# Attention kernel with a weight decode on the side: VectorE's per-head work merged, the decode dealt out by time, seven products on GpSimd

## The chip, the core and the metric

The kernel runs on one core of one Trainium2 chip. The metric is the device time of one execution in microseconds (us), lower is better. Before the change three runs took 588.17, 589.28 and 589.59 us, so the median is 589.28 us.

The engines have short names here as in the profile: PE is TensorE (PEld its weight loads), DVE is VectorE, ACT is ScalarE, POOL is GpSimd, and SP is the engine whose queue issues most DMAs. PSUM is the memory that PE writes its results to, SBUF the main on-chip memory.

## What is computed

Three stages follow each other: an attention with queries pooled in pairs, a mixture of experts in which each token goes to one expert, and a two-layer network. The change touches the first stage and the decode of the weights for the third, which runs beside it.

```python
q_pool = q.reshape(B, H, S // 2, 2, D).mean(axis=3)          # B, H, S, D = 2, 8, 1152, 64
scores = scale * np.matmul(q_pool, k.transpose(0, 1, 3, 2))
scores = scores - np.max(scores, axis=-1, keepdims=True)
attn = np.exp(scores)
attn = attn / (np.sum(attn, axis=-1, keepdims=True) + 1e-09)
x = np.matmul(attn, v)                                        # heads side by side: 1152 tokens x 512
...
skip_score = x @ w_skip ; logits = xc @ w_gate ; e_idx = np.argmax(logits, axis=1)
y[mask] = gate_w[mask, None] * (np.maximum(xc[mask] @ w1[e], 0.0) @ w2[e])
...
h = x @ w_in ; g = h * np.tanh(softplus(h)) ; out = g @ w_out
```

The weights `w_in` and `w_out` arrive in 64-bit numbers. They are turned into 32-bit numbers on the chip, in 32 blocks of 128x512, with integer operations on the high and the low word. This is called the decode here.

## The kernel before

**The iterations.** The attention is a software pipeline of 72 iterations: 8 heads of 9 tiles of 128 queries, and 9 more iterations to run out. `pos` is the number of the iteration within its head (0 to 8), and the tile at `pos` 4 is put together from half tiles of both batches. All work is issued by one Python loop (from line 349) in a fixed order, and each engine runs its own instructions strictly in that order. There is no scheduler.

One iteration `n` issues the following, in this order:

- `turn`: PE transposes the tile of iteration n-3 in 64-column pieces. Eight of nine key blocks go to the PSUM tile `tp`, the ninth to the last columns of `ov`.
- `finish` (only at `pos` 7, for the head before) or `av_step`: PE multiplies transposed weights with the values, two or three of the 18 steps of a head, into the two banks of `ov`. The first nine steps (group 0) fill bank 0, the last nine (group 1) bank 1.
- `ext_copy` (only at `pos` 3): ACT copies the value sums of group 0 out of `ov`. Those of group 1 are copied by DVE inside `av_step`, at `pos` 6.
- `expo`: ACT takes the exponential of the tile of iteration n-1 and sums it.
- `put_e`: ACT copies the transposed pieces out of PSUM. The part from `tp` is issued by `turn`, the part from `ov` after `expo`.
- `scores`: PE computes the scores of tile n into the PSUM tile `s` (4 banks, one buffer). DVE then reads all of `s`, scales it, writes it to SBUF and keeps the extreme value of each row (line 147). This is the eviction, and the next scores wait for its end.
- `dec_run`: DVE gets some operations of the decode.

**`finish`** takes the sums of a finished head (`ext`), multiplies them on PE with a matrix that holds an identity and the gate weights (lines 249 and 256), and DVE divides by the sums of the exponentials (lines 267 and 273, two batches apart). The reciprocals come from `norm`, issued at `pos` 3 of the next head. `logits` adds the gate columns up.

**The decode** of a block has five operations. `first` issues a product of the high word with itself on POOL and a shift on DVE. Two more DVE operations of two inputs each follow (lines 318 and 319), and `last` (line 313) multiplies by the test that the product is not tiny. `DECS` says by `pos` how many operations an iteration gets; in the iteration in which a head's value sums are complete it gets none. Blocks are loaded two ahead from HBM (`dec_load`, first in iteration 6) and stored by SP when the next block begins (`dec_store`). `beside` makes a POOL operation wait for the last score product of the iteration, so that it begins together with the eviction. POOL also adds the query pairs (`q_sum`, two per head).

## Time and profile before

| | |
|---|---|
| median of three runs | 589.28 us (588.17 to 589.59) |
| the profiled execution, its own time | 585.41 us |
| its span, first to last instruction | 583.6 us |
| granted TensorE clock, mean | 0.985 of full speed |
| busy: PE, PEld | 544.4 us (93%), 400.2 us (69%) |
| busy: DVE, ACT, POOL | 376.1 us (64%), 357.5 us (61%), 73.8 us (13%) |
| eviction (line 147), 72 times | 97.7 us, mean 1357 ns |
| exponential (line 158), 72 times | 90.5 us, mean 1257 ns |
| POOL product of the decode (line 307), 32 times | 34.4 us, mean 1075 ns |

The attention fills the first 245 us or so of the span. DVE and ACT are busiest there; the rest is ruled by PE and, in the mixture of experts, by the weight DMAs. A busy PE is not PE at its peak, because matrix products are pipelined and their ends are modelled. The profile says for each idle stretch what ended it, as far as semaphores tell. Where the engine named had long been done, something else ended it.

### The profile page before, as it was taken

Reading aid. Unit: us, or ns where it says so; the run is one execution under the profiler, and the core shown is the slowest. Engines: PE = TensorE matmul, PEld = TensorE weight load, DVE = VectorE, ACT = ScalarE, POOL = GpSimd, SP = SyncE. Lnnn points to the kernel's source line nnn. Section 1 sums busy time; section 2 is a strip of 40 time slices with the busy share of each in tenths; the row PEclk is TensorE's granted clock in tenths of the full one; section 3 lists DMA queues with packets and bytes.
Section 4 is the critical chain, followed back from the end, with each engine's and each line's share of the span. In section 5 each row is a group of like instructions: output and inputs, shape, how many; then the busy total and the mean of one; then the engine's idle time right before and its main releaser. Section 6 shows DMA issues by size and latency. Waiting matters only on the chain. (4 is left out here: it accounts for less than half of the span.)

```text
span 583.6 us, 11993 instructions
## 1 busy us (share of the span) xinstructions
PE 544.4 (93%) x4745; PEld 400.2 (69%) x4745; DVE 376.1 (64%) x731; ACT 357.5 (61%) x663; POOL 73.8 (13%) x82
## 2 busy tenths in 40 slices
PE   6799999999999998779989979999999999999994
PEld 3566666666566665436644645889889999898983
DVE  3588888888888887250010026599987667766663
ACT  3878878788778887202112013599978666676662
POOL 1313231322232220033000100000000000000000
PEclk9999999999999999889998989999999999999998
DMA  8594969798849771029999195346211300010001
GB/s 262 190 311 165 343 210 354 231 326 280 295 140 353 243 269 45 19 83 338 402 361 384 53 342 195 111 148 229 61 36 58 106 2 1 0 56 1 1 0 58
DMA packets 50388, 102.99 MB, mean 176 GB/s; under 512 B 14075, under 2 KB 15483, under 8 KB 50320
## 3 DMA queue, kind: packets, MB, share of 16 engines
q1 hardware_dynamic: 47792, 95.99, 47.7%
q0 software_dynamic: 1296, 3.75, 2.0%
q10 hardware_dynamic: 1232, 2.36, 1.2%
q8 instruction: 41, 0.67, 0.5%
q14 instruction: 27, 0.22, 0.1%
HBM read 85.49 MB, written 17.04 MB: 176 GB/s over the span
## 5 line engine op out<-in xcount | busy, mean ns | idle before, releaser
L147 DVE TENSOR_SCALAR_CACHE_REDUCE scp<-s 128x1152 f32<-128x1152 f32 x72 | 97.7, 1357 | 31.5 <-PE s L144 18.8
L1046 PE MATMUL ph<-xT,wi 128*128 128x384 f32 x576 | 108.5, 337 | 0.0
L1046 PEld LDWEIGHTS ph<-xT,wi 128*128 128x128 f32 x576 | 102.2, 188 | 4.2
L144 PE MATMUL s<-ks,qs 64*128 64x288 f32 (+1 forms) x640 | 89.3, 427 | 8.9 <-DVE scp L147 7.3
L158 ACT ACTIVATE scp<-scp,mx 128x1152 f32<-128x1152 f32 x72 | 90.5, 1257 | 11.2 <-DVE scp L147 10.7
L1100 PE MATMUL po<-wo,gh 128*128 128x512 f32 x288 | 90.3, 394 | 0.8 <-ACT gh L1085 0.6
L206 PE MATMUL ov<-eT,vt 128*64 128x288 f32 x576 | 84.3, 422 | 1.2 <-ACT eT L188 1.2
L188 ACT COPY eT<-tp 128x1024 f32<-128x1024 f32 x64 | 65.0, 1016 | 27.3 <-PE tp L174 27.3
L144 PEld LDWEIGHTS s<-ks,qs 64*128 64x128 f32 (+1 forms) x640 | 48.6, 176 | 44.8 <-DVE scp L147 15.6
L1100 PEld LDWEIGHTS po<-wo,gh 128*128 128x128 f32 x288 | 52.9, 188 | 10.3 <-ACT gh L1085 1.5
L1100 PE MATMUL po<-wo,gl 128*128 128x512 f32 x144 | 57.2, 397 | 0.0
L174 PEld LDWEIGHTS tp<-cst,scp 64*128 64x128 f32 x1152 | 46.9, 138 | 13.7 <-ACT eT L188 3.8
L1070 ACT ACTIVATE u<-u 128x384 f32<-128x384 f32 (+1 forms) x49 | 25.4, 519 | 46.6 <-DVE u L1064 46.1
L1090 DVE TENSOR_TENSOR gl<-s,gh 128x384 fp32r<-128x384 f32 (+1 forms) x49 | 27.0, 550 | 41.7 <-ACT gh L1085 41.5
L206 PEld LDWEIGHTS ov<-eT,vt 128*64 128x64 f32 x576 | 36.6, 138 | 23.0 <-issue 1.4
L307 POOL TENSOR_TENSOR g<-wd 128x512 f32<-128x512 f32 x32 | 34.4, 1075 | 131.6 <-PE s L144 96.3
L174 PE MATMUL tp<-cst,scp 64*128 64x64 f32 x1152 | 48.1, 223 | 0.6 <-ACT eT L188 0.6
L1100 PEld LDWEIGHTS po<-wo,gl 128*128 128x128 f32 x144 | 27.0, 187 | 6.7 <-DVE gl L1090 1.0
L1072 ACT ACTIVATE r<-s,one 128x384 f32<-128x384 f32 (+1 forms) x49 | 30.0, 612 | 1.6
L1071 ACT ACTIVATE s<-u,one 128x384 f32<-128x384 f32 (+1 forms) x49 | 29.9, 610 | 1.6
L1064 DVE TENSOR_SCALAR u<-ph 128x384 f32<-128x384 f32 (+1 forms) x49 | 26.7, 546 | 6.5 <-PE ph L1046 6.4
L1079 DVE SCALAR_TENSOR_TENSOR r<-u,r 128x384 f32<-128x384 f32 (+1 forms) x49 | 26.9, 550 | 1.7
(180 smaller groups left out, 656.3 us busy)
## 6 DMA issues: line engine op xcount, KB each, us to landing
w<-w SPq DMA_DIRECT2D x32, 1024.0 KB, 10.9
wd<-wq SPq DMA_DIRECT2D x32, 512.0 KB, 5.1
wdec<-g SPq DMA_DIRECT2D x32, 256.0 KB, 5.1
vt<-vt SPq DMA_DIRECT2D x8, 576.0 KB, 4.4
ks<-kt SPq DMA_DIRECT2D x15, 288.0 KB, 7.2
ring<-wdec SPq DMA_DIRECT2D x16, 256.0 KB, 4.6
wr<-wdec SPq DMA_DIRECT2D x16, 256.0 KB, 2.8
xr<-qt SPq DMA_DIRECT2D x7, 576.0 KB, 4.7
```

Source lines behind the costliest of these rows:

```text
L144: st["tick"] = nc.tensor.matmul(s[o, half, j, :HQ], w[r], st["k", h, b][r, cs], start=True, stop=True).ins
L147: nc.vector.tensor_scalar(scp.rearrange("p (a c) -> p a c", a=4), s.rearrange("p a j c -> p (a j) c")[:, :, :HQ], -EXP_SCALE, -NEG, op0=AL ...
L158: nc.scalar.activation(scp, scp, AF.Exp, bias=mx, scale=-1.0, accum_out=st["sum", h][:, t : t + 1],)
L174: nc.tensor.matmul(to, e[q, P * i : P * i + P], io["ident"][q, q], start=i < 8 or a != opened, stop=True, is_transpose=True, skip_group_ch ...
L188: nc.scalar.copy(to.rearrange("p k (a c) -> p a k c", a=2), v)
L206: nc.tensor.matmul(acc[D * b : D * b + D, :288], st["v", h][:, b, kc], src[:, kc, b], start=(kc == 0), stop=(kc == KC - 1), skip_group_che ...
L307: beside(nc.gpsimd.tensor_tensor(g, hf, hf, op=ALU.mult))
L1046: nc.tensor.matmul(ph, wi.w[i][:, a, P * k : P * k + P], xTs[c][b][:, k], start=(n == 0), stop=(n == 11),)
L1071: nc.scalar.activation(s[:, c], u[:, c], AF.Square, bias=one)
L1072: nc.scalar.activation(r[:, c], s[:, c], AF.Ln, bias=one)
L1090: nc.vector.tensor_tensor(gl[:, c], a["t"][1][:, c], gh[:, c].bitcast(F32), op=ALU.subtract)
L1100: nc.tensor.matmul(acc[j], g[a][:, P * j : P * j + P], wo[b][:, i], start=(i == 0 and n == 0), stop=(i == 15 and n == 2),)
```

## The change

Five things change in the attention; the stages behind it are the same.

- In `finish` the two batches are divided by one DVE instruction that reads both banks of `ov`, and the four half tiles go to one bank so that one instruction divides them too. `norm` is called in `finish` and no longer at `pos` 3. For the last head ACT has nine columns to scale and not ten.
- `ext_copy` is issued behind `expo` and `put_e`.
- The decode is dealt out by time: each operation has a cost in us (0.45, 0.72, 0.28 for `logits`), and an iteration gives out operations as long as they fit into `SPARE[pos]`. It also does so in the iterations that run out. The first blocks are loaded in iteration 3, not 6.
- For the seven blocks of `OFF` the last operation is not DVE's. POOL does the test and the product, as two instructions.
- POOL's operations are queued in `side` and issued one per iteration. Before a `last`, and before the store of a block of `OFF`, all of them are issued at once.

```diff
-DECS = (2, 2, 2, 2, 2, 2, 2, 3, 3)
+SPARE = (1.45, 1.45, 1.9, 1.45, 1.45, 0.75, 0.0, 1.75, 1.45)
+OFF = (5, 9, 13, 17, 21, 25, 29)
...
         def finish(h):
             st.pop(("v", h))
+            norm(h)
...
-                        xp[b][D * b + 32 * g : D * b + 32 * g + 32, 4 * XW : 5 * XW], ext[q, g, 256:], wb[q],
+                        xp[0][D * b + 32 * g : D * b + 32 * g + 32, 4 * XW : 5 * XW], ext[q, g, 256:], wb[q],
...
-            for b in range(B):
-                nc.vector.tensor_tensor(
-                    xt[:, 5 * b : 5 * b + 4, lo:],
-                    xp[b][:, : 4 * XW].rearrange("p (t c) -> p t c", t=4)[:, :, lo:],
-                    r[:, 5 * b : 5 * b + 4].unsqueeze(2).to_broadcast([P, 4, XW - lo]), op=ALU.mult,
-                )
-                q, x, c = cols[8 + b]
-                nc.vector.tensor_scalar(xt[q, c, lo:], x[:, lo:], r[q, c : c + 1], None, op0=ALU.mult)
...
+            nc.vector.tensor_tensor(
+                xt.rearrange("p (b t) c -> p b t c", b=B)[:, :, :4, lo:],
+                ovs[:, :, : 4 * XW].rearrange("p b (t c) -> p b t c", t=4)[:, :, :, lo:],
+                r.rearrange("p (b t) -> p b t", b=B)[:, :, :4].unsqueeze(3).to_broadcast([P, B, 4, XW - lo]),
+                op=ALU.mult,
+            )
+            nc.vector.tensor_scalar(xt[:, 4, lo:], cols[8][0][:, lo:], r[:, 4:5], None, op0=ALU.mult)
...
             def first():
-                beside(nc.gpsimd.tensor_tensor(g, hf, hf, op=ALU.mult))
+                side.append(lambda: tt(g, hf, hf, op=ALU.mult))
...
+            def third():
+                sts(x1, hb, 0xC0000000, x1, op0=ALU.bitwise_and, op1=ALU.bitwise_or)
+                if i in OFF:
+                    side.append(lambda: nc.gpsimd.tensor_scalar(g, g, W_TINY * W_TINY, None, op0=ALU.is_ge))
+                    side.append(lambda: tt(g, g, x1.bitcast(F32), op=ALU.mult))
+                    dec_out.append((i, g))
+
             def last():
+                while side:
+                    beside(side.pop(0)())
...
-        def dec_run(n):
-            for _ in range(n):
-                if not dec_ops and dec:
+        def dec_run(spare):
+            while dec or dec_ops:
+                if not dec_ops:
...
+                if dec_ops[0][0] > spare:
+                    return
+                cost, op = dec_ops.pop(0)
+                spare -= cost
+                op()
...
         def dec_store():
             if dec_out:
+                while side and dec_out[0][0] in OFF:
+                    beside(side.pop(0)())
...
-            if n % 9 == 3 and n > 9:
-                norm(n // 9 - 1)
...
-            if pos == 3 or not run:
-                ext_copy()
             if 0 < n <= nseq:
                 expo(*seq[n - 1])
             if trn:
                 put_e(*seq[m], slice(8, KC), ovs[:, :, c].unsqueeze(2))
+            if pos == 3 or not run:
+                ext_copy()
...
-                if n == 6:
+                if n == 3:
                     dec_load(0)
                     dec_load(1)
...
-            if run and not fin:
-                dec_run(DECS[pos])
-            if run and sums and (not st["used"] or pos + len(sums) > 8):
-                beside(q_sum(h + 1, sums.pop(0), slice(0, Q), nc.gpsimd))
+            if not fin:
+                dec_run(SPARE[pos] if run else 1.45)
+            if run and not st["used"]:
+                if sums and pos + len(sums) > 7:
+                    beside(q_sum(h + 1, sums.pop(0), slice(0, Q), nc.gpsimd))
+                elif side:
+                    beside(side.pop(0)())
+                elif sums:
+                    beside(q_sum(h + 1, sums.pop(0), slice(0, Q), nc.gpsimd))
```

The order of the instructions is shown at three places. Line numbers of the changed kernel differ a little: its eviction is line 148, its exponential 159, the copies out of PSUM 186 and 189, the copies of the value sums 214 (DVE) and 224 (ACT).

ACT at `pos` 3 of the second head, before: `ext` are the value sums, `eT` the transposed weights, `scp` the scores of a tile.

```order
L188 COPY eT<-tp 128x2x8x64
L223 COPY ext<-ov 128x288
L158 ACTIVATE scp,sums<-scp,mx 128x1152
L188 COPY eT<-ov 128x128
L188 COPY eT<-tp 128x2x8x64
```

And ACT at the same place with the change:

```order
L189 COPY eT<-tp 128x2x8x64
L159 ACTIVATE scp,sums<-scp,mx 128x1152
L189 COPY eT<-ov 128x128
L224 COPY ext<-ov 128x288
L189 COPY eT<-tp 128x2x8x64
```

The copy of the value sums has moved from ahead of the exponential to behind the small copy out of `ov`.

DVE at `pos` 6 to 8 of the third head, where the second head is finished, before: `xt` is the divided output, `r` the reciprocals, `x_...` and `g` belong to the decode.

```order
L213 COPY ext<-ov 128x288
L147 TENSOR_SCALAR scp,mx<-s 128x1152
L267 TENSOR_TENSOR xt<-ov,r 128x292
L273 TENSOR_SCALAR xt<-ov,r 64x73
L267 TENSOR_TENSOR xt<-ov,r 128x292
L273 TENSOR_SCALAR xt<-ov,r 64x73
L147 TENSOR_SCALAR scp,mx<-s 128x1152
L286 TENSOR_TENSOR lg<-lg,xt 128x81
L318 SCALAR_TENSOR_TENSOR x_1021<-wd,x_1021 128x512
L319 SCALAR_TENSOR_TENSOR x_1021<-wd,x_1021 128x512
L147 TENSOR_SCALAR scp,mx<-s 128x1152
```

And DVE at the same place with the change:

```order
L214 COPY ext<-ov 128x288
L148 TENSOR_SCALAR scp,mx<-s 128x1152
L231 TENSOR_SCALAR r<-sums 128x9
L232 RECIPROCAL r<-r 128x9
L265 TENSOR_TENSOR xt<-ov,r 128x2x292
L271 TENSOR_SCALAR xt<-ov,r 128x73
L148 TENSOR_SCALAR scp,mx<-s 128x1152
L284 TENSOR_TENSOR lg<-lg,xt 128x81
L307 TENSOR_SCALAR x_1017<-wd 128x512
L326 SCALAR_TENSOR_TENSOR x_1017<-wd,x_1017 128x512
L148 TENSOR_SCALAR scp,mx<-s 128x1152
```

Four divisions became two, with the two small instructions of `norm` ahead of them. The block that begins here is one of `OFF`: DVE has no last operation for it.

DVE in the first head, before, where the decode begins behind the seventh eviction:

```order
L107 TENSOR_TENSOR qs_138<-xr 128x288
L147 TENSOR_SCALAR scp,mx<-s 128x1152 x7
L308 TENSOR_SCALAR x_306<-wd 128x512
L318 SCALAR_TENSOR_TENSOR x_306<-wd,x_306 128x512
L147 TENSOR_SCALAR scp,mx<-s 128x1152
```

And with the change:

```order
L108 TENSOR_TENSOR qs_138<-xr 128x288
L148 TENSOR_SCALAR scp,mx<-s 128x1152 x4
L307 TENSOR_SCALAR x_214<-wd 128x512
L326 SCALAR_TENSOR_TENSOR x_214<-wd,x_214 128x512
L148 TENSOR_SCALAR scp,mx<-s 128x1152
```

The first operation on a loaded block (`wd`) now stands ahead of the fifth eviction instead of the eighth. On SP the loads of the first three blocks stand where they stood, behind the keys, queries and gate weights of the second head.

## Rows read from the trace of the kernel before

**Rows 1.** Busy time by stage, 74 to 104 us: length, PE, PEld, DVE, ACT, POOL, PEclk, DMA, GB/s

```profile
74.00:104.00 30.00, 29.48 (x372) 19.60 (x370) 26.28 (x46) 24.15 (x41) 8.40 (x7) 1.00 0.80 286
```

**Rows 2.** Timeline of PE, score products at `pos` 8: start us, us, what [idle before]

```profile
29.07 1.24 PE L144 MATMUL s<-ks,qs 64*128 64x288 f32 x8
...
57.76 1.24 PE L144 MATMUL s<-ks,qs 64*128 64x288 f32 x8
...
85.50 1.24 PE L144 MATMUL s<-ks,qs 64*128 64x288 f32 x8
...
226.09 1.24 PE L144 MATMUL s<-ks,qs 64*128 64x288 f32 x8
```

**Rows 3.** Timeline of DVE at `pos` 8 and 0 of the fifth head

```profile
145.70 0.69 DVE L313 SCALAR_TENSOR_TENSOR g<-g,x 128x512 f32<-128x512 f32 x1
146.31 1.35 DVE L147 TENSOR_SCALAR_CACHE_REDUCE scp<-s 128x1152 f32<-128x1152 f32 x1
```

**Rows 4.** Timeline of ACT and PE at `pos` 3 and 4 of the fourth head

```profile
97.49 0.40 ACT L223 COPY ext<-ov 128x288 f32<-128x288 f32 x1 [0.66 <-PE ov L206]
97.79 1.26 ACT L158 ACTIVATE scp<-scp,mx 128x1152 f32<-128x1152 f32 x1
98.21 0.76 PEld L174 LDWEIGHTS tp<-cst,scp 64*128 64x128 f32 x16
...
99.04 0.25 ACT L188 COPY eT<-ov 128x128 f32<-128x128 f32 x1
...
99.34 0.14 PEld L174 LDWEIGHTS ov<-cst,scp 64*128 64x128 f32 x2 [0.37 <-ACT eT L188]
```

**Rows 5.** Timeline of DVE, ACT and PE at `pos` 7 of the fourth head

```profile
109.74 0.46 DVE L267 TENSOR_TENSOR xt<-ov,r 128x292 f32<-128x292 f32 x1 [0.60 <-PE ov L256]
110.15 0.29 DVE L273 TENSOR_SCALAR xt<-ov,r 64x73 f32<-64x73 f32 x1
...
110.36 0.76 PEld L174 LDWEIGHTS tp<-cst,scp 64*128 64x128 f32 x16
...
110.82 0.30 DVE L273 TENSOR_SCALAR xt<-ov,r 64x73 f32<-64x73 f32 x1
...
111.21 0.33 ACT L185 COPY eT<-ov 128x64 f32<-128x64 f32 x2 [0.63 <-DVE xt L273]
...
111.58 0.14 PEld L174 LDWEIGHTS ov<-cst,scp 64*128 64x128 f32 x2 [0.46 <-ACT eT L185]
```

**Rows 6.** Timeline of ACT, PE and DVE where the attention runs out

```profile
231.00 0.40 ACT L223 COPY ext<-ov 128x288 f32<-128x288 f32 x1 [2.12 <-PE ov L206]
...
235.75 6.00 PE L206 MATMUL ov<-eT,vt 128*64 128x288 f32 x36 [1.21 <-ACT eT L188]
...
244.70 0.68 DVE L313 SCALAR_TENSOR_TENSOR g<-g,x 128x512 f32<-128x512 f32 x1
```

**Rows 7.** Busy time by stage, 232 to 240 us, columns as in rows 1

```profile
232.00:236.00 4.00, 1.30 (x22) 1.02 (x24) 0.39 (x2) 3.06 (x7) 0.00 (x0) 0.90 0.01 4
236.00:240.00 4.00, 4.00 (x24) 2.04 (x24) 0.00 (x0) 0.00 (x0) 0.00 (x0) 0.67 0.00 0
```

**Rows 8.** Timeline of SP: first load of the decode is issued

```profile
12.44 0.71 SPq L296 DMA_DIRECT2D wd<-wq  x1
```

**Rows 9.** DMA issues of 12.44 to 13.1 us: count, KB each, us to landing

```profile
wd<-wq SPq DMA_DIRECT2D x1, 512.0 KB, 7.9
```

**Rows 10.** Timeline of DVE, the fifth eviction of the first head

```profile
18.64 1.36 DVE L147 TENSOR_SCALAR_CACHE_REDUCE scp<-s 128x1152 f32<-128x1152 f32 x1 [1.49 <-ACT scp L158]
```

**Rows 11.** Timeline of DVE and POOL where their operations overlap

```profile
33.24 0.69 DVE L313 SCALAR_TENSOR_TENSOR g<-g,x 128x512 f32<-128x512 f32 x1
33.25 1.58 POOL L307 TENSOR_TENSOR g<-wd 128x512 f32<-128x512 f32 x1 [5.15 <-PE s L144]
...
102.04 1.41 POOL L107 TENSOR_TENSOR qs<-xr 128x576 f32<-128x576 f32 x1 [2.29 <-issue]
...
103.31 0.69 DVE L319 SCALAR_TENSOR_TENSOR x<-wd,x 128x512 uint32<-128x512 uint32 x1
```

More of the change, by code (lines that the diff above doesn't have):

```diff
@@ L316, in dec_step @@
             dec_ops.extend((
[L317 to L325 removed]
+                (0.45, first),
+                (0.72, lambda: sts(x1, lb, 29, x1, op0=ALU.logical_shift_right, op1=ALU.bitwise_or)),
+                (0.72, third),
+            ))
+            if i not in OFF:
+                dec_ops.append((0.72, last))
+        side = []
+        def dec_run(spare):
+            while dec or dec_ops:
+                if not dec_ops:
                     i = dec[0][0]
@@ L411, in attention @@
             finish(pend.pop(0))
-        while dec or dec_ops:
-            dec_run(1)
+        dec_run(1e9)
         while dec_out:
```

21 lines of the change are left out of this document (7 added, 14 removed).

## The prediction

> **What bounds the kernel now.** I read the busy time by stage first. In the attention PE is busy for 29.48 of 30 us, DVE for 26.28 and ACT for 24.15 [rows 1]. That says little by itself, since a wait of a few tenths between pipelined products hardly shows. So I went to the timeline and took the start of the score products as the clock of the loop: every iteration has one, and the next cannot start before DVE has evicted this one. The 63 iterations from 29.07 to 226.09 us take 197.02 us, 28.15 us per head of nine. One of these seven heads, from 57.76 to 85.50 us, takes only 27.74 [rows 2]. The reader should see in this that a head has a fixed part, the same in all heads, and a part that comes and goes. I looked for both.
>
> The part that comes and goes is DVE. At `pos` 8 of the fifth head the third decode operation begins at 145.70, and the eviction behind it starts only when it is through, at 146.31 [rows 3]. The scores that it takes were ready 0.6 us earlier.
>
> The fixed part holds two waits of PE. At `pos` 4 the transposes into `ov` wait 0.37 us for ACT's small copy [rows 4]. ACT is late because at `pos` 3 it stood idle for 0.66 us until PE was through with the value products, copied the sums for 0.40 us, and only then took the exponential, at 97.79. At `pos` 8 the same transposes wait 0.46 us for ACT again, and ACT waits 0.63 us for DVE's four divisions [rows 5]. After these waits are taken off, PE works without a gap, so I take PE's own work as the floor.
>
> **The sum, part by part.** All times are of the profiled execution, 585.41 us, which is 0.66% below the median of 589.28. I take the difference off the median.
>
> *Copy of the value sums.* Behind the change the exponential can start when ACT became idle, 97.49 less 0.66 = 96.83, its copy follows 1.25 later (97.79 to 99.04) at 98.08, and the sums are copied by about 98.75. PE's transposes into `ov` can follow those into `tp`, whose loads end at 98.21 + 0.76 = 98.97. So the wait of 0.37 goes, and what is late next is nothing: 0.2 us are left between the copy and the transposes. Seven heads have it: -2.6 us.
>
> *Merged divisions.* The chain runs from 109.74 to 111.12. 292 columns cost 0.46 and, by the eviction (1152 columns in 1.36), each further column about 1 ns; 584 columns then cost about 0.76. The second instruction starts 0.05 before the first ends, as now, and takes 0.3: the end is at 110.75, 0.37 earlier. `norm` is two instructions on nine columns. Two divisions of 73 columns bound them at 0.6, and DVE is idle for 0.60 just ahead of this chain, waiting for PE, so they cost nothing; without that cover they would cost up to 0.4. With ACT 0.37 earlier, PE's wait of 0.46 shrinks to about 0.1. Seven heads: -2.6 us.
>
> *Decode by time.* An iteration now gets at most two decode operations between evictions, 1.44 us in all. With the eviction's 1.36 that is 2.8 us, and an eviction and its scores alone (1.36 and 1.24, one after the other) already need 2.6 and their hand-overs, about 2.8. Nothing in a head then makes an eviction late, and each head runs like the best one: 197.02 - 7 x 27.74 = 2.8 us. Seven of 32 last operations leave DVE, 0.69 each, but that time is idle time now and adds nothing. Taken: -2.8 us. The bounds are 0 and -2.8.
>
> *Running out.* At 231.00 the sums were copied after ACT had been idle for 2.12 us, and the last exponential stood behind the copy [rows 6]. It fits into that idle time. Its 1.26 us leave the chain, of which PE's transposes give back some 0.25: the last value products start 1.0 earlier than 235.75. Their 6.00 us hold a second loss. PE was busy for only 1.30 of the 4 us before, the granted clock fell from 1.00, and from 236 to 240 its mean was 0.67, between the levels of 2.4 and 1.2 GHz, with PE busy throughout: 4 x 0.33 = 1.3 us [rows 7]. With a gap shorter by one microsecond I expect the clock to hold: -1.3, bounds 0 and -1.5. At the end DVE has no decode operation left ahead of the routing (0.68 at 244.70), two divisions less and ACT one column less, but DMAs of the output rows run beside: -0.5, bounds -0.2 and -0.9. Together -2.8 us.
>
> *Earlier start of the decode.* This one costs. SP issues the first load of the decode at 12.44 [rows 8], in a queue whose order the change keeps up to there, and it lands 7.9 us later, at 20.34 [rows 9]. Before, its first reader on DVE stood behind the seventh eviction and never waited. Now that reader stands in DVE's queue ahead of the fifth eviction, which started at 18.64 [rows 10]. The eviction waits for the load and for two operations (0.46 and 0.6 from start to start), until 21.4: +2.8 us, and PE, ACT and the next scores wait with it. PE has no value products yet in this head, so it stands for these 2.8 us and for its usual gap. By the 1.30 of 4 us above [rows 7] the clock falls there too, and one set of score products, 1.24 us, runs at half speed: +1.2, bounds 0 and +1.5. Together +4.0 us.
>
> *GpSimd.* POOL's test and product for a block of `OFF` are both issued at `pos` 8. The test runs beside the eviction, the product after DVE's third operation, so beside other DVE work. What such an overlap costs the trace shows twice. POOL took 1.58 us where DVE had started 0.01 earlier on two SBUF operands, against a mean of 1.08 in the table; so POOL waits. Where POOL was first, until 103.45, DVE's operation of 103.31 still took 0.69 [rows 11]: DVE lost nothing. By these rows the cost is zero. The Trainium skill (SBUF — State Buffer, "Who interferes with whom") says that VectorE and GpSimd lock a shared port pair for a whole instruction, and whoever comes second is held entirely. The first pair of rows agrees with that, the second does not show it. By the rule the product waits for DVE's shift and ends some 3.35 us behind the start of the eviction, the next square follows until 4.4, and DVE's next operation, due at 4.13, is held for some 0.2 us: +1.4 in seven heads. I take 0 and keep +1.4 as a bound. The test itself has no row, POOL never ran a one-operand instruction on 512 columns here; the product's 1.08 is the nearest, and up to about 1.8 us the following eviction hides it.
>
> The sum: -2.6 - 2.6 - 2.8 - 2.8 + 4.0 = -6.8 us, 578.6 for a profiled execution and **582.5 us** for the median.
>
> **Rivals.**
>
> *The load costs nothing (chance 0.12).* If the load landed by 17 us, or the stalled head caught up later, the +4.0 would go: -10.8, 578.5 us. For it: only one landing is seen, and this early part of the head has PE gaps of a microsecond. Against: the gaps are there because the eviction loop itself is the limit, so it has nothing to catch up with.
>
> *The waits move (0.16).* PE's waits at `pos` 8 and DVE's late evictions are replaced by another wait, for instance for POOL's queue or for the copy of the value sums, which would miss the transposes if it were 0.2 later. Then only the first term and the end remain: -2.6 - 2.8 + 4.0 = -1.4, 587.9 us. For it: PE is busy nearly all the time and all three engines are close to each other. Against: the best head shows no such wait.
>
> *GpSimd holds VectorE (0.07), slower than before.* If POOL's test of 512 columns is slow and holds DVE's third operation at `pos` 8, the next eviction is late. It begins about 2.85 us after the last; behind the test DVE has 0.6 and 0.4 to do. So it is late from a test of 1.8 us on, and from 3.0 us on (1.2 late in each of seven heads, 8.4) all gains are gone. With a test of 3.5 us it would be 1.7 x 7 = 11.9 - 6.8 = +5.1, 594.4 us. For it: no row has its price, and the overlap is real [rows 11]. Against: 1.08 us for two operands. The Trainium skill (GPSIMD Engine Reference, "Elementwise — side-by-side cycle accounting") gives about 1 cycle per element for one operand, by which my estimate of the test is about half a microsecond, and the sum stays.
>
> **How the numbers follow.** The forecast gets 0.65. Its own range goes from -8.6 (no fall of the clock in the first head, -1.2, and the end at its bounds, -0.6) to -2.7 (half of DVE's part, +1.4, the clock falls at the end as before, +1.3, and +1.4 for the port), 580.7 to 586.6. With the first rival and part of the second the range is 578.0 to 587.0 us. A difference under 0.3%, 1.8 us, can't be told from none. Faster by more: the forecast and the first rival, and half of the second, 0.85. Within: half of the second, 0.08. Slower: the third, 0.07.
>
> **What would show it.** In the new profile the fifth eviction of the first head should start near 21.4 us behind a DVE operation that waits for a DMA, and the granted clock should dip right after. Score starts at `pos` 8 should be 27.0 us apart in every head. The wait for ACT's copy at `pos` 4 should be gone, and that at `pos` 8 be near 0.1. The last value products should take 4.6 us, not 6.0. POOL's product should overlap DVE without making its operations longer. I am wrong if the heads keep differing from each other, if a head is longer than 27.5 us, or if no stall is seen in the first head.

## The result and the profile after

The changed kernel takes 579.72 us, the median of 4 runs (575.43 to 581.50), against 588.72 us of the kernel before in 4 runs: a ratio of 0.9874 with a 95% interval of 0.9838 to 0.9909, 1.3% faster. The forecast was 582.5 us, the range 578.0 to 587.0. The profiled execution, the fastest of the four, took 575.43 us with a span of 573.6, 10.0 us shorter than the span before.

To see where these went I cut the span at events on PE that every execution has: the first score products, those at `pos` 8 of the first head, the last score products, the last value products, their end, and the transposes of the first gathered rows. All times in us, from the timeline of PE.

| stage | before | after | difference | predicted |
|---|---|---|---|---|
| start to first score products | 5.97 | 5.30 | -0.67 | |
| first head, to its `pos` 8 | 23.10 | 25.11 | +2.01 | +4.0 |
| 63 iterations | 197.03 | 188.57 | -8.46 | -8.0 |
| last score products to last value products | 9.66 | 8.60 | -1.06 | -1.0 |
| last value products | 6.00 | 4.59 | -1.41 | -1.3 |
| to the transposes of the gathered rows | 12.34 | 11.78 | -0.56 | -0.5 |
| the rest, which the change does not touch | 329.53 | 329.60 | +0.07 | |
| span | 583.6 | 573.6 | -10.0 | -6.8 |

The heads come first. The timeline of PE after the change shows the score products at `pos` 8, as [rows 2] did before:

```profile
30.41 1.24 PE L145 MATMUL s<-ks,qs 64*128 64x288 f32 x8
...
57.30 1.24 PE L145 MATMUL s<-ks,qs 64*128 64x288 f32 x8
...
84.19 1.24 PE L145 MATMUL s<-ks,qs 64*128 64x288 f32 x8
...
218.98 1.24 PE L145 MATMUL s<-ks,qs 64*128 64x288 f32 x8
```

The spacing is 26.89 us in five of the seven heads and 27.02 and 27.09 in the other two; before it was 27.74 to 28.69. In the stretch of [rows 1], PE is now busy without a gap (the columns are length, PE, PEld, DVE, ACT, POOL, PEclk, DMA share, GB/s):

```profile
74.00:104.00 30.00, 30.00 (x376) 20.09 (x376) 25.36 (x44) 25.50 (x44) 11.29 (x10) 1.00 0.76 271
```

The two waits of PE are gone. This is the timeline of ACT, PE and DVE of the changed kernel, first `pos` 3 and 4, then `pos` 7 and 8 of the fourth head, against [rows 4, 5]:

```profile
95.51 1.26 ACT L159 ACTIVATE scp<-scp,mx 128x1152 f32<-128x1152 f32 x1
...
96.90 0.76 PEld L175 LDWEIGHTS tp<-cst,scp 64*128 64x128 f32 x16
96.91 0.40 ACT L224 COPY ext<-ov 128x288 f32<-128x288 f32 x1
...
97.57 0.15 PEld L175 LDWEIGHTS ov<-cst,scp 64*128 64x128 f32 x2
...
107.84 0.77 DVE L265 TENSOR_TENSOR xt<-ov,r 128x584 f32<-128x584 f32 x1
...
108.53 0.28 DVE L271 TENSOR_SCALAR xt<-ov,r 128x73 f32<-128x73 f32 x1
...
108.90 0.33 ACT L186 COPY eT<-ov 128x64 f32<-128x64 f32 x2
...
109.28 0.14 PEld L175 LDWEIGHTS ov<-cst,scp 64*128 64x128 f32 x2
```

The copy of the value sums (L224) now follows the exponential, and the loads for the transposes into `ov` at 97.57 carry no wait, where they had 0.37 us. The division chain runs from 107.84 to 108.81, 0.97 us in place of the 1.38 from 109.74 to 111.12, and the loads at 109.28 carry no wait either, where they had 0.46.

In the run-out (timeline of PE; then the busy time by stage, columns as above) the last value products answer to [rows 6, 7]:

```profile
227.58 4.59 PE L207 MATMUL ov<-eT,vt 128*64 128x288 f32 x36 [1.21 <-ACT eT L189]
```

```profile
224.00:228.00 4.00, 1.96 (x40) 1.45 (x38) 3.84 (x5) 2.81 (x6) 2.62 (x2) 1.00 0.20 70
228.00:232.00 4.00, 4.00 (x36) 2.16 (x32) 1.61 (x3) 0.00 (x0) 0.00 (x0) 1.00 0.18 66
```

PE's granted clock stayed at 1.00 (2.4 GHz), so the 36 products took 4.59 us and not 6.00.

The first head went otherwise than predicted. Timeline of DVE and POOL, to be held against [rows 10]; then the busy time by stage:

```profile
16.91 1.36 DVE L148 TENSOR_SCALAR_CACHE_REDUCE scp<-s 128x1152 f32<-128x1152 f32 x1 [2.48 <-PE s L145]
18.01 1.04 POOL L306 TENSOR_TENSOR g<-wd 128x512 f32<-128x512 f32 x1 [8.02 <-DMA wd<-wq]
...
18.20 1.14 DVE L307 TENSOR_SCALAR x<-wd 128x512 uint32<-128x512 uint32 x1
...
19.37 0.69 DVE L326 SCALAR_TENSOR_TENSOR x<-wd,x 128x512 uint32<-128x512 uint32 x1
...
19.98 1.35 DVE L148 TENSOR_SCALAR_CACHE_REDUCE scp<-s 128x1152 f32<-128x1152 f32 x1
```

```profile
11.00:13.00 2.00, 1.97 (x13) 1.66 (x15) 0.00 (x0) 1.31 (x2) 0.00 (x0) 0.59 1.03 385
13.00:14.00 1.00, 0.99 (x19) 0.80 (x15) 0.94 (x1) 0.08 (x1) 0.00 (x0) 0.50 1.03 371
```

The load was there when POOL began at 18.01, 2.3 us earlier than it had landed before, so the fifth eviction started at 19.98 and not at 21.4. But the granted clock was already at 0.50 (1.2 GHz) from 13 us on, before the decode had an operation, with PE mostly idle just before; the third and fourth score products took 2.0 and 2.3 us instead of 1.24. So the first head lost 2.0 us, most of it by another way than I had worked out: the spacing of the score products is 1.8 us longer in all behind the third and fourth of them, where the clock is low, than in a head without such losses (22.84 us in e1 and e2 below), and only 0.2 us longer behind the fifth, where the load was to cost. By the prediction's own sign, "if no stall is seen in the first head", this step was wrong for this execution. Whether that is the change or this one execution was the first question for the experiments.

### The profile page after: what moved, and what is told of

Its sections match the earlier page's. It is cut to its first block, busy times and chain, and to the rows that moved or that the text cites. A ratio compares the mean times of both kernels' runs of the same rounds, so it can differ in the third digit from the quotient of the medians.

```text
span 573.6 us, 11983 instructions
## 1 busy us (share of the span) xinstructions
PE 538.6 (94%) x4745; PEld 398.4 (69%) x4745; DVE 371.1 (65%) x708; ACT 358.1 (62%) x662; POOL 93.3 (16%) x96
## 3 DMA queue, kind: packets, MB, share of 16 engines
q0 software_dynamic: 1296, 3.75, 2.2%
## 4 chain that ended last, share of the span: by engine, by line
PE 28%; issue 7%; DMA 7%; DVE 6%; ACT 2%; DVEq 0%; ACTq 0%; POOLq 0%; SPq 0%
PE po L1119 14%; PE ph L1065 14%; DMA ytok<-xr,sidx 4%; DMA ytok<-yg,sidx 2%; DVE wi L964 1%; DMA yt<-ytok 1%; DVE wo L1054 1%; DVE u L1083 1%; DVE r L1098 1%; DVE gl L1109 1%; DVE u L1097 1%; PE ft L1015 0%; PE ft L1027 0%; DMA wr<-wdec 0%; ACT r L1091 0%
## 5 line engine op out<-in xcount | busy, mean ns | idle before, releaser
L145 PE MATMUL s<-ks,qs 64*128 64x288 f32 (+1 forms) x640 | 91.1, 432 | 7.4 <-DVE scp L148 5.7
L207 PE MATMUL ov<-eT,vt 128*64 128x288 f32 x576 | 82.9, 416 | 1.2 <-ACT eT L189 1.2
```

What stands on the lines that cost most here:

```text
L145: st["tick"] = nc.tensor.matmul(s[o, half, j, :HQ], w[r], st["k", h, b][r, cs], start=True, stop=True).ins
L207: nc.tensor.matmul(acc[D * b : D * b + D, :288], st["v", h][:, b, kc], src[:, kc, b], start=(kc == 0), stop=(kc == KC - 1), skip_group_che ...
```

## The experiments

My theory was that of the prediction: four gains that are independent of each other, less what the early start of the decode costs. The rivals were that the waits only move, that GpSimd holds VectorE, and that the slow first head is chance. The table gives each kernel's ratio to the kernel before and the stages as above, in us; "first" is the first head to its `pos` 8, "63" the iterations from there, "to AV" and "AV" the way to the last value products and these, "to gather" the next stage. The "ninth score start" of the expectations is counted from zero: it lies one iteration (2.85 us) behind the end of "first".

| run | ratio | 95% interval | start | first | 63 | to AV | AV | to gather | rest |
|---|---|---|---|---|---|---|---|---|---|
| before | | | 5.97 | 23.10 | 197.03 | 9.66 | 6.00 | 12.34 | 329.5 |
| after | 0.9874 | 0.9838 to 0.9909 | 5.30 | 25.11 | 188.57 | 8.60 | 4.59 | 11.78 | 329.6 |
| e0 after again | 0.9856 | 0.9811 to 0.9900 | 5.77 | 31.30 | 188.59 | 8.60 | 6.23 | 11.67 | 330.3 |
| e1 copy alone | 0.9917 | 0.9881 to 0.9953 | 5.70 | 22.84 | 193.98 | 8.60 | 6.02 | 12.36 | 333.3 |
| e2 divisions alone | 0.9947 | 0.9913 to 0.9982 | 5.97 | 22.84 | 194.46 | 9.89 | 6.98 | 12.29 | 328.3 |
| e3 decode by time alone | 0.9979 | 0.9950 to 1.0009 | 5.97 | 23.52 | 193.82 | 9.66 | 6.11 | 15.02 | 329.9 |
| e4 all last products on DVE | 0.9898 | 0.9844 to 0.9952 | 5.29 | 26.83 | 188.26 | 8.60 | 6.28 | 13.90 | 333.5 |
| e5 late start | 0.9833 | 0.9796 to 0.9870 | 5.40 | 22.84 | 188.30 | 8.59 | 4.59 | 13.01 | 332.2 |
| e6 test twice | 0.9992 | 0.9963 to 1.0022 | 5.26 | 26.64 | 194.34 | 8.60 | 4.59 | 11.86 | 330.6 |
| e7 late start, fills | 0.9800 | 0.9767 to 0.9833 | 5.38 | 22.83 | 188.29 | 8.60 | 4.59 | 12.09 | 329.9 |
| e8 e7 without fills | 0.9795 | 0.9766 to 0.9824 | 5.75 | 23.00 | 188.27 | 8.59 | 4.59 | 12.07 | 329.1 |
| e9 copy and fills | 0.9888 | 0.9860 to 0.9916 | 5.97 | 22.90 | 193.95 | 8.60 | 4.59 | 12.49 | 328.8 |
| e10 e7 again | 0.9795 | 0.9764 to 0.9826 | 5.97 | 23.16 | 188.27 | 8.59 | 4.59 | 12.02 | 329.2 |

Two things should be read from it first. The column "63" repeats to a few hundredths between executions of the same code, so it prices a part of the change that the total cannot. The column "rest" is the same code in all rows and spreads over 5 us; that is why single totals differ as they do.

### e0: the changed kernel once more

> The changed kernel once more, to see what of its profile belongs to the one execution. In the first profile the granted clock was 0.50 from 13 to 17 us and the first head took 1.34 us longer than before, though the predicted wait for the decode's load was not seen. Theory A (the clock there is this execution's, not the change's): the clock reads 1.00 from 11 to 17 us, the fifth score products start near 17.5 us, and then the fifth eviction waits for the load, by as much as that lands after 17.5 us: with a landing at 20.3 us the eviction starts near 21.4. Theory B (the change itself lowers the clock): half clock again, fifth score products near 18.4 us, no eviction more than 0.5 us late. Both: the 63 iterations from the ninth score start on take 188.6 us within 0.5, ratio 0.984 to 0.991.

The kernel is unchanged. The 1.34 us of the expectation are counted from the start of the span (30.41 against 29.07); from the first score products it is the 2.01 of the table. Theory A held in this execution, and the stall of the prediction is there in full: DVE and POOL in the timeline, then PE, then the busy time by stage.

```profile
20.58 0.43 DVE L307 TENSOR_SCALAR x<-wd 128x512 uint32<-128x512 uint32 x1 [3.90 <-DMA wd<-wq]
20.70 1.21 POOL L306 TENSOR_TENSOR g<-wd 128x512 f32<-128x512 f32 x1 [9.83 <-DMA wd<-wq]
21.04 1.41 DVE L326 SCALAR_TENSOR_TENSOR x<-wd,x 128x512 uint32<-128x512 uint32 x1
...
22.38 1.35 DVE L148 TENSOR_SCALAR_CACHE_REDUCE scp<-s 128x1152 f32<-128x1152 f32 x1
...
23.79 2.29 PE L145 MATMUL s<-ks,qs 64*128 64x288 f32 x8 [5.05 <-DVE scp L148]
```

```profile
21.00:23.00 2.00, 0.00 (x0) 0.00 (x0) 1.97 (x3) 0.00 (x0) 2.00 (x2) 0.89 0.18 68
23.00:25.00 2.00, 1.22 (x6) 0.94 (x8) 1.89 (x4) 1.24 (x2) 0.71 (x1) 0.50 0.01 2
...
35.00:37.00 2.00, 2.00 (x12) 0.80 (x10) 1.64 (x4) 2.00 (x3) 0.00 (x0) 0.69 0.03 8
```

DVE's first decode operation waits 3.90 us for the load, and the eviction behind it starts at 22.38, 1.0 later than I had said, since the second operation took 1.41 us beside POOL's product and not 0.69. PE stands idle for 5.05 us; then the granted clock falls to 0.50 and comes back only at 36 us. "First" is 8.5 us above the 22.84 of an undisturbed head, half of it the stall, half the clock. In e4 and e6, which keep the early start, the first operation waited 2.04 and 1.93 us for the load, and "first" is 4.0 and 3.8 us above. So the four profiles with the early start show +2.3, +8.5, +4.0 and +3.8 us, a mean of 4.6.

Not all of that is the load. By the spacing of the score products from the fifth on, the load and what follows from it cost 0.2, 8.5, 2.3 and 2.2 us, a mean of 3.3. The rest of the first, third and fourth is the early fall of the clock, which e4 and e6 show again (0.59 and 0.58 from 11 to 13 us), and later second score products. And in e4 and e6 the clock does not fall behind the wait. In e4 (timeline of PE, then busy time by stage):

```profile
23.11 1.24 PE L145 MATMUL s<-ks,qs 64*128 64x288 f32 x8 [3.19 <-DVE scp L148]
```

```profile
23.00:25.00 2.00, 1.81 (x26) 1.43 (x26) 1.87 (x5) 1.62 (x4) 0.60 (x2) 1.00 0.22 39
```

So the predicted +4.0 lies within a wide spread, and its second part, 1.2 us for the clock behind the wait, was seen in one profile of four.

### e1, e2, e3: one part of the change at a time

e1 puts only the copy of the value sums behind the exponential and its copy:

```diff
-            if pos == 3 or not run:
-                ext_copy()
             if 0 < n <= nseq:
                 expo(*seq[n - 1])
             if trn:
                 put_e(*seq[m], slice(8, KC), ovs[:, :, c].unsqueeze(2))
+            if pos == 3 or not run:
+                ext_copy()
```

> Before, with the copy of the value sums moved behind the exponential and its copy, nothing else. Theory A (the terms are independent): the wait of the transposes at the fifth iteration of a head goes, seven heads by 0.37 to 0.45 are 2.6 to 3.1 us of the 197.0 us of the 63 iterations (194.2), and in the run-out the last value products start 1.0 us earlier and take 4.6 instead of 6.0 us, 2.4 in all; together 5.0 to 5.5 us, ratio 0.991. Rival (the waits move): DVE's late evictions take the place of the removed wait, the 63 iterations stay within 0.7 of 197.0, and only the run-out's 2.4 us are left, ratio 0.996.

e2 takes only the new `finish`: the small products all go into `xp[0]`, one division covers the eight tiles, and `norm` moves into it:

```diff
-                        xp[b][D * b + 32 * g : D * b + 32 * g + 32, 4 * XW : 5 * XW], ext[q, g, 256:], wb[q],
+                        xp[0][D * b + 32 * g : D * b + 32 * g + 32, 4 * XW : 5 * XW], ext[q, g, 256:], wb[q],
```

> Before, with the merged divisions alone. Theory A: the chain of the divisions is 0.37 us shorter, the wait of the transposes at the last iteration of a head falls from 0.46 to about 0.1 us, the 63 iterations take 194.4 us, ratio 0.9955. Rival (the waits move): DVE still has three decode operations in that iteration, so the eviction takes the place of the wait and the 63 iterations take over 196 us, ratio 0.998 or more.

e3 takes only the dealing by time, without GpSimd and with the start of before:

```diff
+SPARE = (1.45, 1.45, 1.9, 1.45, 1.45, 0.75, 0.0, 1.75, 1.45)
+OFF = ()
...
-                dec_run(DECS[pos])
+                dec_run(SPARE[pos] if run else 1.45)
```

> Before, with the decode dealt out by time, all last products on VectorE, its loads and its start where they were. Theory A: no eviction is late for a decode operation, the heads are alike and each like the best one of before, 27.74 us, the 63 iterations take 194.2 us; of the four operations per block some are left over at the end, which costs nothing if they are done by the time the last exponential needs DVE, ratio 0.995. Rival 1 (DVE's lateness was caught up within the head): the 63 iterations take over 196 us, ratio 0.998 to 1.000. Rival 2 (without GpSimd the leftover grows): the 63 iterations take 194 us, but more than ten decode operations stand behind the last eviction and the routing starts later, ratio 1.00 or more.

The 63 iterations got shorter by 3.05, 2.57 and 3.21 us, 8.83 together; all in one, as in e5, it is 8.73. The terms add, and "the waits move" has fallen. Each sits where the prediction put it: with e1 the iteration at `pos` 4 falls from 3.29 to 2.85 us, with e2 that at `pos` 8 from 3.83 to between 3.44 and 3.55, and with e3 the varying iterations at `pos` 1 and 7 become 2.85 and 2.89 in every head, so that all seven heads take 27.69 us (the best one of before had 27.74). What e1 was expected to gain in the run-out came only in part: its last value products start 1.06 us earlier behind the last score products, but take 6.02 us and not 4.6.

e3 alone is not faster as a whole: its interval includes 1. The end of the attention says why, and it is what the second rival says, though that had put the ratio at 1.00 or more. The blocks on DVE leave four decode operations behind the last division, ahead of the routing (timeline of DVE):

```profile
241.86 0.24 DVE L287 TENSOR_TENSOR lg<-lg,xt 128x81 f32<-128x81 f32 x1
242.02 0.42 DVE L310 TENSOR_SCALAR x<-wd 128x512 uint32<-128x512 uint32 x1
242.48 0.69 DVE L329 SCALAR_TENSOR_TENSOR x<-wd,x 128x512 uint32<-128x512 uint32 x1
243.20 0.69 DVE L315 SCALAR_TENSOR_TENSOR x<-wd,x 128x512 uint32<-128x512 uint32 x1
...
243.99 0.69 DVE L324 SCALAR_TENSOR_TENSOR g<-g,x 128x512 f32<-128x512 f32 x1
```

The routing begins 2.0 us later behind the last value products than before, and "to gather" is 2.7 us longer in all, which takes back most of the 3.2. So the room that an earlier start makes for the decode has a use, only not in the heads: nothing may be left at the end.

### e4, e6: what GpSimd's part is worth and what it could cost

e4 empties the list of blocks:

```diff
-OFF = (5, 9, 13, 17, 21, 25, 29)
+OFF = ()
```

> The changed kernel with the last products of all blocks on VectorE (OFF empty). Theory A (the seven blocks on GpSimd buy nothing in the heads): GpSimd's test and product no longer run beside VectorE, the 63 iterations are as long or up to 0.5 us shorter than with them (188.1 to 188.6), and the ten decode operations behind the last eviction still end before the value sums are copied, so that the end is the same; ratio to before 0.982 to 0.990. Rival (VectorE needs the room): without GpSimd an eviction is late in some iterations, the 63 take over 189.5 us or the leftover work makes the routing later by a microsecond or more, ratio 0.990 or more.

Theory A held for the heads: 188.26 us without the seven products on GpSimd, 0.3 less than with them. That 0.3 is not a fixed price of GpSimd, though, since e5, e7, e8 and e10 have 188.3 with it; it is the two heads of 27.02 and 27.09 us, in which one eviction each is late, and which the shifts of the decode in these runs remove. In the first of the two GpSimd has a part: a small cast on DVE, due once in the program, takes 0.31 us beside POOL's square (at 143.49 us) and not 0.22, and the next eviction is 0.1 us late. The cause of the other I leave open. At the end the last decode operation was through well before the value sums were copied, as expected. So with the early start the seven products on GpSimd bought nothing that these runs show. "To gather" is 2.1 us longer in this execution; the routing's operations on VectorE take about 6.6 us as after the change, and what is longer lies at GpSimd, which issues the gather of the rows 3.6 us behind their index in place of 1.5. Nothing in the profile ties it to the decode, and I leave it open. The ratio does not tell e4 from the changed kernel.

e6 issues GpSimd's test twice, the first time into a spare tile:

```diff
+                    side.append(lambda: nc.gpsimd.tensor_scalar(j, g, W_TINY * W_TINY, None, op0=ALU.is_ge))
                     side.append(lambda: nc.gpsimd.tensor_scalar(g, g, W_TINY * W_TINY, None, op0=ALU.is_ge))
```

> The changed kernel with GpSimd's test issued twice for each of the seven blocks (the first into a spare tile), which lengthens GpSimd's work there from 1.5 + 1.3 to 3.0 + 1.3 us. It prices the prediction's third rival, by which a test longer than 1.8 us makes an eviction late. Theory A (the port lock holds VectorE): the product and the next square move 1.5 us back, against VectorE's three decode operations, whose times rise from 0.69 to 0.8 to 1.6 us, and in seven heads an eviction is late by 0.5 to 1.2 us: the 63 iterations take 192 to 197 us, ratio to before 0.992 or more. Rival (GpSimd's work only moves into other idle time): the 63 iterations stay within 0.7 of 188.6 us, ratio 0.983 to 0.990.

Theory A held: the 63 iterations took 194.34 us, 5.8 more, and with the loss in the first head the kernel is as slow as before. Timeline of POOL, then of DVE, from `pos` 8 of the third head on:

```profile
87.89 1.49 POOL L315 TENSOR_SCALAR j<-g 128x512 f32<-128x512 f32 x1 [2.52 <-PE s L145]
89.46 1.62 POOL L316 TENSOR_SCALAR g<-g 128x512 f32<-128x512 f32 x1
91.16 1.27 POOL L317 TENSOR_TENSOR g<-g,x 128x512 f32<-128x512 f32 x1
92.40 2.93 POOL L306 TENSOR_TENSOR g<-wd 128x512 f32<-128x512 f32 x2
```

```profile
91.97 1.01 DVE L328 SCALAR_TENSOR_TENSOR x<-wd,x 128x512 uint32<-128x512 uint32 x1
93.02 1.42 DVE L312 SCALAR_TENSOR_TENSOR x<-wd,x 128x512 uint32<-128x512 uint32 x1
94.35 1.35 DVE L148 TENSOR_SCALAR_CACHE_REDUCE scp<-s 128x1152 f32<-128x1152 f32 x1
```

The product and the squares behind it now fall on DVE's next two operations, which take 1.01 and 1.42 us in place of 0.69 each, and POOL's two squares 2.93 in place of 2.08. The eviction at `pos` 1, here at 94.35, is late in six heads, by 0.8 us in five and by 1.9 in one. So the third rival is a real mechanism. For a test of 3.0 us I had worked out 8.4 us; with two of 1.5 it is 5.8, and the late eviction is the second behind the one that the test runs beside, not the next.

In the changed kernel the same overlap just stays harmless. Timeline of POOL and of DVE at `pos` 8 of the second head:

```profile
58.73 1.49 POOL L314 TENSOR_SCALAR g<-g 128x512 f32<-128x512 f32 x1 [2.53 <-PE s L145]
...
59.87 0.69 DVE L312 SCALAR_TENSOR_TENSOR x<-wd,x 128x512 uint32<-128x512 uint32 x1
...
60.71 1.32 POOL L315 TENSOR_TENSOR g<-g,x 128x512 f32<-128x512 f32 x1 [0.49 <-DVE x L312]
...
61.99 1.04 POOL L306 TENSOR_TENSOR g<-wd 128x512 f32<-128x512 f32 x1
...
62.80 0.77 DVE L326 SCALAR_TENSOR_TENSOR x<-wd,x 128x512 uint32<-128x512 uint32 x1
```

The test takes 1.49 us and the product waits until DVE's shift is done. One DVE operation becomes 0.08 us longer, and no eviction is late for it.

### e5: the decode starts late again

```diff
-                if n == 3:
+                if n == 6:
                     dec_load(0)
```

> The changed kernel with the decode's first loads and first operations at the seventh iteration, as before the change. Theory A (the earlier start costs): the ninth score start comes at 31.4 to 32.4 us as in the four profiles with the late start, not at 33.3 and 39.9 as in the two of the changed kernel; the 63 iterations stay at 188.6. In exchange six decode operations more are left at the end and three of them stand ahead of the routing, 2.1 us. Net 0 to -6 us against the changed kernel, ratio to before 0.977 to 0.986. Rival (the slow first head is chance, it hits any kernel): the ninth score start stays above 33 us or the fifth eviction waits here as well, ratio 0.988 or more.

Theory A held but for two sizes. The ninth score start came at 31.1 us, 0.3 ahead of the expected window, since the first score products began early, at 5.40. "First" is 22.84 us, as in e1 and e2, the 63 iterations are 188.30, and three decode operations stand ahead of the routing. The routing begins 2.0 us later for them, near the 2.1 expected, but "to gather" is only 1.3 us longer (13.01 against 11.7 on the mean of the changed kernel's two profiles), since GpSimd issued the gather 0.45 us behind the index here and 1.5 there. The ratio is 0.9833. Its interval overlaps that of the changed kernel, so the total alone does not show the gain; the stages do, and e7, e8 and e10 repeat it.

### e7 to e10: the run-out, and a version that is faster than both

e7 starts the decode at the sixth iteration, deals out four operations per iteration of the run-out, and fills PE's two idle stretches there with eight small matmuls on zeros:

```diff
+            if trn and not run and m > nseq - 3:
+                keep_warm(nc, io, s[:, 0, 0], (3, 5)[m - nseq + 2])
...
-                if n == 3:
+                if n == 5:
...
-                dec_run(SPARE[pos] if run else 1.45)
+                dec_run(SPARE[pos] if run else 2.9)
```

> The changed kernel with three edits: the decode starts at the sixth iteration, four decode operations instead of two are dealt out per iteration of the run-out, and eight small matmuls with zeros (three and five) fill the two idle stretches of TensorE of 0.8 and 1.2 us ahead of the last value products. Theory A: no wait for the load in the first head (ninth score start 31.4 to 32.4 us); no decode operation ahead of the routing; TensorE has no gap, the granted clock stays at 1.00 through the run-out, and the last value products take 4.6 us, where five of six profiles so far show 6.0 to 7.0. Ratio to before 0.975 to 0.982, 2 to 5 us better than the changed kernel. Rival (the clock does not fall for the gap): the granted clock falls below 0.9 between the last scores and the end of the value products all the same and these take 6 us or more; ratio 0.980 to 0.986.

e8 is e7 without the small matmuls, e10 is e7 again, and e9 is e1 with the small matmuls alone:

> The run that starts the decode at the sixth iteration and deals out four operations per iteration of the run-out, without the eight small matmuls, to see what these do. Both theories: ninth score start 31.0 to 31.2 us after a first score start near 5.4, 63 iterations 188.3 us, no decode operation ahead of the routing. Theory A (the clock falls in some executions, for the gaps): in the profile the granted clock may fall in the run-out (then the last value products take 6.0 to 6.3 us) or not (4.6); over the runs the median is 0.3 to 1.5 us above that with the matmuls. Rival (the matmuls change nothing): medians within 0.3 us. A difference of this size is under what the comparison can tell, so the profile's clock counts more than the medians. Ratio to before 0.977 to 0.985.

> Before with the copy of the value sums moved, and the eight small matmuls (three and five) in TensorE's idle stretches of 0.8 and 1.2 us of the run-out. With the copy alone the granted clock fell to 0.57 and 0.50 behind these stretches and the last value products took 6.0 us. Theory A (the clock falls for the idle time ahead of it): with the stretches filled it stays at 1.00 and the value products take 4.6 us, starting 8.6 us behind the last score products as without the matmuls; ratio to before 0.987 to 0.993. Rival (it falls for another reason): below 0.9 in the run-out again and 6 us.

> The kernel with the decode from the sixth iteration, four decode operations per iteration of the run-out and the eight small matmuls once more, for a second interval and a second profile. Theory A (what it showed belongs to the kernel): median within 0.3% of 575.1 us, ratio to before 0.977 to 0.983, first head 25.7 us from the first to the tenth score start, granted clock 1.00 in the run-out, last value products 4.6 us. Rival (the first profile was lucky): the first head takes over 27 us or the value products 6 us.

e7, e8 and e10 have ratios of 0.9800, 0.9795 and 0.9795 with intervals that end at 0.983: 2.0% below before, and 0.6 to 0.8% below the two results of the changed kernel. They lie below the interval of the first of these and overlap that of e0. "First" is 22.8 to 23.2, and no decode operation is left ahead of the routing. "To gather" is 12.0 to 12.1, 0.3 over the changed kernel: DVE's last decode operation ends 0.5 us behind the last value products, and the copy of the value sums waits for it. This is the version I would use, and e8 suffices for it: between e8 and e10, which ran beside the same runs of the kernel before, the medians are 572.46 and 573.41 us and the ratios the same. That is neither theory's margin, and no gain of the matmuls can be seen.

What the matmuls do could show only where the clock falls without them. In e1 the last value products took 6.02 us, with a granted clock of 0.83 and 0.74 in the two stretches behind the last scores (busy time by stage):

```profile
228.00:232.00 4.00, 1.95 (x26) 1.30 (x26) 0.00 (x0) 2.36 (x4) 0.00 (x0) 0.83 0.01 4
232.00:236.00 4.00, 4.00 (x27) 2.08 (x25) 0.00 (x0) 0.00 (x0) 0.00 (x0) 0.74 0.00 0
```

The same stretches of e9, the same kernel with the idle time filled:

```profile
228.00:232.00 4.00, 3.85 (x45) 1.97 (x42) 0.00 (x0) 2.65 (x5) 0.00 (x0) 1.00 0.01 4
232.00:236.00 4.00, 4.00 (x34) 2.12 (x30) 0.00 (x0) 0.00 (x0) 0.00 (x0) 1.00 0.00 0
```

The clock stays at 1.00 and the products take 4.59 us. With the stretches filled it stayed in three profiles of three (e7, e9, e10). With them idle it stayed in four of six that have the other edits of the change, and fell in all four with at most one of them (before, e1, e2, e3). That would fit a fall for the idle time ahead of it, but these runs do not show it. e0 to e3 ran on one chip, e4 to e7 on a second and e8 to e10 on a third. On the first the clock fell in all four, on the third it stayed in all three, in e8 with the stretches idle. So the difference of e1 and e9 may also be that of the chips or of the executions, and why the same idle time is borne in one execution and not in the next is open.

## Why the prediction was right, step by step

*What bounds the kernel* was right: PE has no gap left in the stretch of [rows 1], and what was gained came from waits of a few tenths in front of PE's own work, read from the spacing of the score products.

*Copy of the value sums*: right, a little too small. Predicted -2.6, measured -3.05 in e1. I multiplied the recorded wait of 0.37 us by seven; the whole iteration became 0.45 shorter. The spacing of the score products was the better measure than the wait that is put down to one instruction.

*Merged divisions*: right, -2.6 against -2.57 in e2. The sizes of the two divisions (0.76 and 0.3 predicted, 0.77 and 0.28 measured) were right as well.

*Decode by time*: right, -2.8 against -3.2 in e3. The bound "each head runs like the best one" was passed by 0.05 us per head. What I did not say is that this part gives nearly all of it back at the end unless the decode also gets room elsewhere; that follows from e3's four operations ahead of the routing.

*Running out*: the first part was right (-1.06 against -1.0), and so was the end (-0.56 against -0.5). The step "with a gap shorter by one microsecond I expect the clock to hold" was no more than likely. It held in the profile of the change, but in e0 and e4 it fell and the products took 6.23 and 6.28 us, and in e1, whose gap is as short, it fell too. So the upper bound of 0 was passed by up to 0.3. In the six profiles that have the other edits of the change and idle stretches there, the clock stayed in four, so the forecast should have carried about two thirds of the term.

*Earlier start of the decode*: the wait was right, the clock behind it was not, and the size was not one number. The predicted chain (an operation of DVE that waits for the load, the eviction behind it, PE idle, the clock at half) stands row by row in e0, with 22.38 us for an eviction that I had put at 21.4; the waits in e4 and e6 give 21.70 and 21.48. The last link, the clock, held in e0 alone: in e4 and e6 PE stood idle for 3.19 and 3.07 us and the clock read 1.00 behind it. In the profile that came with the result the load landed at 18.0 us, not at 20.34, and there the stall is nearly absent, as the first rival has it. I saw one landing [rows 9] and took it as the kernel's. What the load cost in the four profiles, 0.2 to 8.5 us, is wider than the bounds I set. Two terms were missing: DVE's second operation is held by POOL's square (1.41 us in e0, e4 and e6, where I had 0.6), and in e0 the clock stays down until about 36 us, which costs 4.3 us and not 1.2.

One piece stays open. In three of the four profiles with the early start the granted clock fell to 0.6 at 11 to 13 us, before any decode operation, and in none of the nine with the later start did it fall in the first head at all. Nothing that I found in the rows links a decode operation that is still to come to a clock at that time, and I do not call the change its cause. The rows show two more things. The ten matmuls that warm PE up at the start of every kernel here took 3.72 to 3.75 us in these three profiles and 3.83 to 4.43 in all others, so the three differ from the rest before any work that the change touches. And idle time just ahead does not tell them apart: from 9 to 11 us PE was busy for 0.51 us in the profile after and for 0.48 in e5, whose clock stayed at 1.00.

*GpSimd*: "the sum stays" was right for the cost, wrong for the reason. I read [rows 11] as showing that POOL waits and DVE loses nothing. The profile after has DVE's shift at 1.14 us in place of 0.42, and in e0 its second operation at 1.41 in place of 0.69, where POOL had started first. That is what the Trainium skill says (SBUF — State Buffer, "Who interferes with whom"): the two engines lock a shared port pair, and whoever comes second waits. The trace agrees in these rows. It does not for a DVE operation that begins in POOL's last 0.2 us: at 62.80 that became only 0.08 longer with 0.23 of POOL's product to run, and the row of [rows 11] that misled me was of this kind. The test's price, for which I had a bound of 1.8 us, is 1.49. The Trainium skill (GPSIMD Engine Reference, "Elementwise — side-by-side cycle accounting") led to an estimate of about half a microsecond; the trace does not agree.

*Rivals.* That the waits move fell with e1, e2 and e3. That the load costs nothing is nearly true for the one profile and for no other. That GpSimd holds VectorE was shown as a mechanism by e6, with a longer test; at the size used it made one eviction 0.1 us late.

*The sum.* I said -6.8 us and the profiled pair showed -10.0, the medians -9.0. The differences are in the terms that vary: the first head cost 2.0 in place of 4.0 in that execution, the heads gained 0.5 more, and the first score products came 0.7 us earlier. In e0 the same code came out only 1.2 us under the span of before, since the first head took 8.2 us longer and the last value products did not gain. So the four gains in the heads and the run-out were worked out, but that the total came so near the forecast is in part luck: between the two profiles of the changed kernel the first head moves by 6.2 us and the last value products by 1.6.

## What to carry to other kernels

Price a change in a pipelined loop by the spacing of one event per iteration, position by position: it repeats to hundredths where totals spread by several microseconds, and terms that sit at different positions add. When an operation is moved ahead of work that everyone waits for, look at what it reads: a load whose landing was never waited for has no known landing time, and one profile shows one draw of it (here DVE or POOL could begin on it between 18.0 and 20.6 us). Work that is dealt into idle time has to be all gone by the end, so count what stands ahead of the next stage, and move it into time where its engine idles rather than to an earlier start.

## What the runs showed that I had not expected

GpSimd's test of one operand on 512 columns (1.49 us) is slower than its product of two operands on as many (1.32 us for two tiles, 1.04 us for the square of one).

VectorE and GpSimd slow each other when both work on two operands from SBUF without pause: in the run-out of the changed kernel DVE's second, third and fourth operations take the following (timeline of DVE), against 0.69 us each.

```profile
222.62 1.65 DVE L326 SCALAR_TENSOR_TENSOR x<-wd,x 128x512 uint32<-128x512 uint32 x1
...
224.30 1.41 DVE L312 SCALAR_TENSOR_TENSOR x<-wd,x 128x512 uint32<-128x512 uint32 x1
...
225.81 1.36 DVE L321 SCALAR_TENSOR_TENSOR g<-g,x 128x512 f32<-128x512 f32 x1
```

POOL's two squares beside them took 2.94 us in place of 2.08. It cost nothing here, since DVE's next work waits for the last value products until 232 us.

In e0, after PE had stood idle for 5 us, the granted clock stayed at 0.50 (1.2 GHz) from 23 until about 36 us, over three sets of score products and the first value products. There the stall cost about as much again in clock (4.3 us) as in time (4.2). In e4 and e6, with PE idle for 3.19 and 3.07 us at the same place, the clock cost nothing.
